# First weights issued from ScalarE's queue, and twelve buffers for raw inputs in an attention and Fourier filter kernel

## The chip, the cores and the metric

The kernel runs as one launch on one core of a Trainium2 chip. The metric is device time in microseconds (us) of one execution, as the median of several runs. Before the change it is 635.23 us, the median of 3 runs (634.75 to 635.24).

In the text PE is TensorE (PEld its weight loads), DVE is VectorE, ACT is ScalarE, POOL is GpSimd and SP is SyncE. SP computes nothing here; it issues DMAs. ACT and POOL can issue DMAs too, each from a queue of its own.

## What is computed

Two independent parts share the core, and their outputs are concatenated. Part A is attention with 16 heads of 28 channels, in which all heads share one key and one value head; part B filters an image of 2048 x 448 in the frequency domain.

```python
def _A_ref(x, wq, wk, wv, wo):
    q = (x @ wq).reshape(B, S, H, Dh).transpose(0, 2, 1, 3)
    k = x @ wk
    v = x @ wv
    scores = jnp.einsum("bhqd,bkd->bhqk", q, k) * (Dh ** -0.5)
    p = _softmax(scores, axis=-1)
    o = jnp.einsum("bhqk,bkd->bhqd", p, v)
    return o.transpose(0, 2, 1, 3).reshape(B, S, H * Dh) @ wo
...
def _B_ref(x, w_r, w_i):
    X = jnp.fft.rfft2(x, axes=(-2, -1)) * (w_r + 1j * w_i)
    return jnp.fft.irfft2(X, s=(S, D), axes=(-2, -1))
```

B is 1, S 2048, D 448, H 16 and Dh 28; all inputs are f32.

## The kernel before

The work has a start of some 70 us and a long main part. The main part (`PLAN`, line 48, and the loop at line 895) is written out by hand: PE computes scores (line 918), ACT takes their exponentials (853, 929, 943), PE multiplies them with the values (864), and the steps of the Fourier filter are set between them. The order on PE is the order of the program text in the whole kernel; the orders on DVE and ACT are fixed by hand only from line 506 on. Ahead of it a scheduler that comes with the language orders every other engine's instructions by its own estimate of when they can run.

The start, lines 257 to 502, makes the queries, keys and values. x is split in four columns of 512 positions (`c`), and its 448 channels in four blocks of 128 rows (`j`, `NK` = 4; the last block holds 64 channels twice). Matmuls in full f32 precision are put together from three products of numbers in a shorter format: `split_w` (335) makes the parts `wqh` and `wql` of a weight block, `split_x` (342) the parts `xh` and `xl` of an input block, `proj` (353) does the products. The high parts are casts, on ACT but for the very first block of x, which DVE casts (345). The low parts are differences on DVE (340, 349, 351). `evac` (361) writes a result to `qraw` on ACT and takes its largest magnitude on DVE (`qmx`, 364).

Every raw block lands in a buffer named `raw` of 128 x 512 f32 (256 KB), of which there are eight; a ninth load waits until the first buffer has been read. All raw loads are issued by SP, in this order: the first block of x (312); the first block of `wq` in three pieces of 128, 128 and 256 columns (321); the first block of the second column of x; then for j = 1, 2, 3 a block of x and the block of `wq` in two halves (328). Then come the rest of the second column, constants, the inputs `xb` and `fw` of the Fourier filter's first step (118, 120), and the third column of x.

A DMA is also given one of eight semaphores in turn, and it waits until the DMA that had the same semaphore before has landed. So at most eight DMAs of SP and ACT together are under way.

While the first loads are under way, ACT loads its function table and runs one exponential on a dummy (298), and PE runs 16 matmuls on zeros (305, `WARM` = 10, 6). PE's first real product is one of `xh` with the first piece of `wqh`; then one more matmul on zeros; then the products with `xl` and `wql`.

Beside the projections the start does the first step of the Fourier filter in eight parts: `fft1_fold` (123) adds and subtracts blocks of `xb` on DVE, PE multiplies the result (155), ACT copies it (161), PE multiplies again (174), and SP stores it (189). Near its end come four steps that lead to the first scores: `qm`, the largest magnitudes of the keys' part of `qraw` (459, DVE), with PE's `key_max` behind it (379); `prod` and `shift` (286, 291, 292), which make the constants `cvec`; `build_q(0, 0)`, three operations on DVE that make `ql`, `qh` and again `ql` (232, 234, 223); and `copy_q`, which spreads these over `qa` by DVE (210), ACT (208), SP and POOL (211). The first scores (918) read `qa`. POOL meanwhile fetches rows of keys and values to `kf` (273).

Of the kernel before, what the change touches and what calls it, by code (L numbers as in the profile page):

```python
# [10 lines left out]
F32 = mybir.dt.float32  # L11
# [54 lines left out]


WARM = 10, 6


@with_exitstack
def kernel(ctx: ExitStack, tc: tile.TileContext, t: dict):
    nc = tc.nc
# [183 lines left out]
    with tc.tile_pool(name="w1", bufs=1) as w1:  # L257
# [35 lines left out]

        halves = slice(0, 1024), slice(1024, 2048)
        with tc.tile_pool(name="x1", bufs=2) as x1:
            warm = x1.tile([1, 1], F32, name="warm")
            nc.vector.memset(warm, 0.0)
            nc.scalar.activation(warm, warm, AF.Exp)
# [3 lines left out]
            def zeros(n, nothing=None):  # L302
                nothing = bank() if nothing is None else nothing
                for _ in range(n):
                    mm(nothing[:, :256], idle[:, :128], idle, start=True, stop=True)

            for n in WARM:
                zeros(n)

            def raw(src, eng):  # L310
                r = x1.tile([128, 512], F32, name="raw", bufs=8)
                eng.dma_start(r, src)
                return r


            first = slice(0, 128), slice(128, 256), slice(256, 512)
            xr, wr = {}, {}
            xr[0, 0] = raw(t["xa"][0, :, 0], nc.sync)
            wr[0] = x1.tile([128, 512], F32, name="raw", bufs=8)
            for s in first:  # L320
                nc.sync.dma_start(wr[0][:, s], t["wq"][:, 0, s])

            xr[1, 0] = raw(t["xa"][1, :, 0], nc.sync)
            for j in range(1, NK):
                xr[0, j] = raw(t["xa"][0, :, j], nc.sync)
                wr[j] = x1.tile([128, 512], F32, name="raw", bufs=8)
                for s in (slice(0, 256), slice(256, 512)):
                    nc.sync.dma_start(wr[j][:, s], t["wq"][:, j, s])

# [647 lines left out]
    for k in range(4):  # L977
        divide(c, NG - 1, k)
        s = slice(128 * k, 128 * k + 128)
# [17 lines left out]
    with tc.If(rv > int(np.float32(BOUND).view(np.int32))), tc.tile_pool(name="g1", bufs=1) as g1:  # L997
# [13 lines left out]
        with tc.For_i(0, 64, 1) as n:  # L1011
# [3 lines left out]
            for i in range(4):  # L1015
                r = slice(32 * i, 32 * i + 32)
# [14 lines left out]
        with tc.For_i(0, NC, 1) as nq:  # L1031
            y = g1.tile([128, 4, D], F32, name="y")
            nc.vector.memset(y, 0.0)
            with tc.For_i(0, NG, 1) as ng:
# [5 lines left out]
                for i in range(4):  # L1040
                    r = slice(32 * i, 32 * i + 32)
# [145 lines left out]
```

## Time and profile before

| what | value |
| --- | --- |
| median of 3 runs | 635.23 us (634.75 to 635.24) |
| the profiled execution | 635.08 us |
| its span, first to last instruction | 633.3 us |
| granted clock of TensorE, mean | 1.00 |
| ACT, idle while PE computes what it evacuates at L363, 0 to 75 us | 15.4 us in 10 waits |
| ACT, idle for raw blocks of x (L347), 0 to 75 us | 4.6 us in 6 waits |
| ACT, idle for raw weights (L339), 0 to 75 us | 3.0 us in 4 waits |
| DVE, idle for the first block of x (L345) | 2.9 us |
| bytes moved by DMA | 66.74 MB, mean 105 GB/s |

Times in the rows of a profile are microseconds from the start of the span. A row in order of time gives the start, the length, the engine, the line, the operation, what is written and what is read, and in brackets the engine's idle time ahead of it with what ended it. "SPq", "ACTq" and "POOLq" rows are DMAs being issued; the data move later. A list of waits gives for each waiting line its releaser, the sum, the count and the longest wait. DMA share is the mean busy share of the 16 DMA engines.

### The profile page before, as it was taken

To read this page: it belongs to the slowest core of one execution; us is meant where nothing else is said; L and a number is where in the kernel's file an instruction comes from. 1 tells how busy PE (TensorE), PEld (TensorE's weight loads), DVE (VectorE), ACT (ScalarE), POOL (GpSimd) and SP (SyncE) were. 2 spreads that over 40 slices of the span, in tenths; PEclk is the share of its full clock that TensorE was granted. 3 is DMA by queue.
4 is the path that set the end of the run, shared out by engine and by line. 5 is a ranking of instruction groups with operands and counts; after the bars stand their busy time and mean duration, and the time that the engine had idled before them with its cause. 6 is when DMAs were issued, how large, how long until landed. Compare 5 with 4: busy or idle time off the path is not lost. (4 is left out here: it accounts for less than half of the span.)

```text
span 633.3 us, 12165 instructions
## 1 busy us (share of the span) xinstructions
PE 627.4 (99%) x4437; PEld 377.7 (60%) x4437; DVE 439.9 (69%) x793; ACT 546.9 (86%) x984; POOL 61.5 (10%) x118
## 2 busy tenths in 40 slices
PE   9999999999999999999999999999999999999997
PEld 7877645646565655646565665565566565555555
DVE  5999648789998943866766845277687764457653
ACT  5554999999999998988989989998989989989991
POOL 4021501011113110000110100001010100000000
PEclk9999999999999999999999999999999999999999
DMA  8865863456455522216340513034152413030011
GB/s 254 288 177 168 261 167 87 115 146 177 124 152 124 139 65 66 76 64 187 77 106 18 125 37 82 16 83 147 35 129 60 98 55 91 16 82 11 21 31 61
DMA packets 37891, 66.74 MB, mean 105 GB/s; under 512 B 8009, under 2 KB 22746, under 8 KB 36860
## 3 DMA queue, kind: packets, MB, share of 16 engines
q1 hardware_dynamic: 32608, 52.50, 30.2%
q0 software_dynamic: 4640, 12.48, 7.7%
q8 instruction: 36, 0.59, 0.4%
q10 hardware_dynamic: 576, 0.92, 0.4%
q14 instruction: 31, 0.25, 0.1%
HBM read 29.81 MB, written 17.87 MB: 75 GB/s over the span
## 5 line engine op out<-in xcount | busy, mean ns | idle before, releaser
L853 ACT ACTIVATE p<-s 128x512 f32<-128x512 f32 x405 | 222.1, 638 | 27.3 <-PE s L918 26.5
L918 PE MATMUL s<-qa,ka 128*128 128x512 f32 x756 | 227.6, 402 | 0.0
L918 PEld LDWEIGHTS s<-qa,ka 128*128 128x128 f32 x756 | 138.1, 188 | 60.9 <-issue 26.8
L924 DVE COPY k<-s 128x512 f32<-128x512 f32 x122 | 80.1, 684 | 62.9 <-PE s L918 62.7
L864 PE MATMUL s<-p,vs 128*32 128x512 f32 x976 | 121.3, 595 | 0.0
L853 ACT ACTIVATE qraw<-s 128x512 f32<-128x512 f32 x137 | 79.2, 655 | 6.5 <-PE s L918 6.5
L943 ACT ACTIVATE k<-k 128x1024 f32<-128x1024 f32 x80 | 83.5, 1145 | 0.0
L864 PEld LDWEIGHTS s<-p,vs 128*32 128x32 f32 x976 | 29.4, 109 | 64.3 <-issue 59.4
L918 PE MATMUL sx<-qa,ka 128*128 128x512 f32 x137 | 55.3, 403 | 0.0
L918 PE MATMUL po<-qa,ka 128*128 128x512 f32 x131 | 53.2, 406 | 0.0
L853 ACT ACTIVATE p<-po 128x512 f32<-128x512 f32 x75 | 48.2, 642 | 4.5 <-PE po L918 4.2
L864 PE MATMUL s<-qraw,vs 128*32 128x512 f32 x384 | 49.5, 593 | 0.0
L853 ACT ACTIVATE p<-sx 128x512 f32<-128x512 f32 x64 | 41.5, 649 | 3.0 <-PE sx L918 2.9
L738 POOL DMA_DIRECT2D ol<-ol x36 | 18.0, 508 | 229.0 <-DVE ol L761 156.9
L864 PE MATMUL s<-k,vs 128*32 128x512 f32 x304 | 39.7, 594 | 0.0
L918 PEld LDWEIGHTS sx<-qa,ka 128*128 128x128 f32 x137 | 25.7, 188 | 11.1 <-issue 4.2
L918 PEld LDWEIGHTS po<-qa,ka 128*128 128x128 f32 x131 | 24.6, 188 | 11.3 <-issue 5.0
L868 DVE STREAM_TRANSPOSE osb<-s 128x512 f32<-128x512 f32 x13 | 9.3, 716 | 28.0 <-PE s L864 27.9
L864 PEld LDWEIGHTS s<-qraw,vs 128*32 128x32 f32 x384 | 12.0, 110 | 27.3 <-issue 26.1
L924 DVE COPY k<-po 128x512 f32<-128x512 f32 x17 | 11.6, 685 | 21.4 <-PE po L918 21.3
L853 ACT ACTIVATE qraw<-sx 128x512 f32<-128x512 f32 x35 | 22.9, 653 | 2.0 <-PE sx L918 2.0
L924 DVE COPY p<-s 128x512 f32<-128x512 f32 x35 | 23.0, 681 | 0.0
(277 smaller groups left out, 973.5 us busy)
## 6 DMA issues: line engine op xcount, KB each, us to landing
qa<-qa SPq DMA_DIRECT2D x15, 512.0 KB
raw<-xa SPq DMA_DIRECT2D x16, 256.0 KB
xb<-xb SPq DMA_DIRECT2D x8, 512.0 KB
qa<-qh SPq DMA_DIRECT2D x64, 64.0 KB
qa<-ql SPq DMA_DIRECT2D x60, 64.0 KB
t<-bs SPq DMA_DIRECT2D x16, 225.0 KB
wr<-wr POOLq DMA_DIRECT2D x16, 225.0 KB, 3.8
wi<-wi POOLq DMA_DIRECT2D x16, 225.0 KB, 5.2
```

The costliest lines, as they stand in the source:

```text
L738: nc.gpsimd.dma_start(ol[c][o, g].bitcast(F32), ol[c][r, 0].bitcast(F32))
L853: nc.scalar.activation(tiles[-1][:, h % 2], sc, AF.Exp, scale=SCALE)
L864: mm(po[c, g][32 * i:32 * i + 32], vs[:, kc], ps[i // 2][:, i % 2], start=(n == 1), stop=(n == 16))
L868: nc.vector.transpose(o, po[c, g])
L918: begun.append(mm(sc, ka[:, kc * 128:(kc + 1) * 128], qa[c, g][:, h], start=True, stop=True))
L924: nc.vector.tensor_copy(keep[i][h // 2][:, h % 2], sc)
L943: nc.scalar.activation(p, p, AF.Exp, scale=SCALE)
```

## The change

The three pieces of the first weight block are issued from ACT's queue, as the first things that ACT does, in place of SP's. The constant `RAW` sets the number of `raw` buffers, twelve where there were eight.

```diff
+RAW = 12
...
         with tc.tile_pool(name="x1", bufs=2) as x1:
+            first = slice(0, 128), slice(128, 256), slice(256, 512)
+            xr, wr = {}, {}
+            wr[0] = x1.tile([128, 512], F32, name="raw", bufs=RAW)
+            for s in first:
+                nc.scalar.dma_start(wr[0][:, s], t["wq"][:, 0, s])
             warm = x1.tile([1, 1], F32, name="warm")
             nc.vector.memset(warm, 0.0)
             nc.scalar.activation(warm, warm, AF.Exp)
...
-                r = x1.tile([128, 512], F32, name="raw", bufs=8)
+                r = x1.tile([128, 512], F32, name="raw", bufs=RAW)
...
-            first = slice(0, 128), slice(128, 256), slice(256, 512)
-            xr, wr = {}, {}
             xr[0, 0] = raw(t["xa"][0, :, 0], nc.sync)
-            wr[0] = x1.tile([128, 512], F32, name="raw", bufs=8)
-            for s in first:
-                nc.sync.dma_start(wr[0][:, s], t["wq"][:, 0, s])
...
-                wr[j] = x1.tile([128, 512], F32, name="raw", bufs=8)
+                wr[j] = x1.tile([128, 512], F32, name="raw", bufs=RAW)
```

PE's order is the same. On the other engines the scheduler's order changes too. Lines in the rows of the change are higher by one in most places, since it adds a line in the middle of the program.

The beginning of ACT's order, before and then with the change (`wq` is the weight matrix in memory, `xa` the input, `wqh` and `xh` the high parts):

```order
L1183 UNCONDITIONAL_BRANCH
L298 ACT_TABLE_LOAD
L298 ACTIVATE warm<-warm 1x1
L339 ACTIVATE wqh<-raw 128x128 x2
L339 ACTIVATE wqh<-raw 128x256
```
```order
L1184 UNCONDITIONAL_BRANCH
L301 DMA raw<-wq 128x128 x2
L301 DMA raw<-wq 128x256
L304 ACT_TABLE_LOAD
L304 ACTIVATE warm<-warm 1x1
L340 ACTIVATE wqh<-raw 128x128 x2
L340 ACTIVATE wqh<-raw 128x256
```

The three issues stand ahead of the table load, and what follows is as it was. On SP they are gone, and the next loads follow the first block of x directly.

DVE's order at the first query, before and with the change (`cvec` holds the constants, `ql` and `qh` the parts of the query, the rows with `f` and `xb` are pieces of a fold, `qmx` a largest magnitude):

```order
L364 TENSOR_REDUCE qmx<-qraw 128x1
L292 COPY cvec<-s_89 128x4
L130 TENSOR_TENSOR f<-xb 113x16x32
L232 TENSOR_SCALAR ql<-qraw,mask,cvec 128x512
L130 TENSOR_TENSOR f<-xb 113x16x32
L234 CAST qh<-ql 128x512
L132 TENSOR_TENSOR xb<-f 113x512
L223 TENSOR_TENSOR ql<-ql,qh 128x512
L133 TENSOR_TENSOR xb<-f 113x512
```
```order
L365 TENSOR_REDUCE qmx<-qraw 128x1
L131 TENSOR_TENSOR f<-xb 113x16x32
L293 COPY cvec<-s_89 128x4
L131 TENSOR_TENSOR f<-xb 113x16x32
L233 TENSOR_SCALAR ql<-qraw,mask,cvec 128x512
L133 TENSOR_TENSOR xb<-f 113x512
L235 CAST qh<-ql 128x512
L134 TENSOR_TENSOR xb<-f 113x512
L224 TENSOR_TENSOR ql<-ql,qh 128x512
```

A piece of the fold moved from behind each of the four steps to ahead of it. Ahead of `qm` (459) DVE has the same instructions as before, some in another order.

POOL's order around the copies of `ql`, before and with the change (`kf` holds keys and values, `wr` a later weight of the filter):

```order
L273 DMA kf<-qraw 4x1536 x7
L273 DMA kf<-qraw 4x512 x5
L211 DMA qa<-ql 32x512 x2
L273 DMA kf<-qraw 4x512 x2
L211 DMA qa<-ql 32x512 x2
L593 DMA wr<-wr 64x900 x2
```
```order
L274 DMA kf<-qraw 4x1536 x7
L274 DMA kf<-qraw 4x512 x5
L212 DMA qa<-ql 32x512
L274 DMA kf<-qraw 4x512 x2
L212 DMA qa<-ql 32x512 x3
L594 DMA wr<-wr 64x900 x2
```

The last two fetches of `kf` now stand ahead of three of the four copies of `ql`, before ahead of two.

## The prediction

> **What bounds the kernel now.** I read the page first, for the shares of the engines, then the waits of PE, then the stretch from 0 to 70 us in order of time: the change lies there, and a wait that PE does not feel is worth nothing.
>
> ```profile
> span 633.3 us, 12165 instructions
> PE 627.4 (99%) x4437; PEld 377.7 (60%) x4437; DVE 439.9 (69%) x793; ACT 546.9 (86%) x984; POOL 61.5 (10%) x118
> ```
> ```profile
> PE s L305 <- DVE idle L301: 1.1, 1, 1.1
> PE s L379 <- DVE qm L459: 0.7, 1, 0.7
> ```
> ```profile
> 629.10 0.36 PE L971 MATMUL po<-wol,oh 128*128 128x448 f32 x1
> ```
>
> PE is idle for 633.3 - 627.4 = 5.9 us in all. Of this 633.3 - 629.46 = 3.8 us lie behind its last matmul (the last output), 1.1 us ahead of the first warm-up matmul, and 0.7 us in one hole at L379, where PE waits for DVE's `qm`. An earlier load can therefore win only the hole and what PE loses at its start. Those rows come next.
>
> ```profile
> 1.11 3.60 PE L305 MATMUL s<-idle 128*128 128x256 bf16 x16 [1.11 <-DVE idle L301]
> 4.51 0.29 PEld L359 LDWEIGHTS s<-xh,wqh 128*128 128x128 f32 x1 [0.28 <-ACT wqh L339]
> 4.52 0.72 PE L359 MATMUL s<-xh,wqh 128*128 128x512 f32 x1
> 5.16 0.50 PE L359 MATMUL s<-xl,wqh 128*128 128x512 f32 x1
> 5.50 0.40 PE L359 MATMUL s<-xh,wql 128*128 128x512 f32 x1
> 5.73 0.40 PE L359 MATMUL s<-xh,wqh 128*128 128x512 f32 x1
> 53.99 0.61 PE L379 MATMUL s<-qm,sel 128*128 128x1 f32 x4 [0.73 <-DVE qm L459]
> 69.64 2.24 PE L918 MATMUL s<-qa,ka 128*128 128x512 f32 x8
> ```
>
> The warm-ups hold PE from 1.11; the first real matmul starts at 4.52 and the second at 5.16; from 5.50 on they follow each other every 0.23 us, and the list of waits has nothing more until the hole that ends at 53.99. So in the first 54 us two chains run side by side: PE from its start, with 0.73 us to spare at the hole, and DVE up to `qm`, which decides when the hole ends. DVE's rows:
>
> ```profile
> 3.95 0.43 DVE L345 CAST xh<-raw 128x512 fp32r<-128x512 f32 x1 [2.90 <-DMA raw<-xa]
> 4.41 0.69 DVE L349 TENSOR_TENSOR xl<-raw,xh 128x512 fp32r<-128x512 f32 x1
> 15.76 0.69 DVE L351 TENSOR_TENSOR xh<-raw,xh 64x512 fp32r<-64x512 f32 x1 [0.44 <-ACT xh L347]
> 17.43 1.29 DVE L130 TENSOR_TENSOR f<-xb 113x512 f32<-113x512 f32 x2 [0.98 <-DMA xb<-xb]
> 53.78 0.16 DVE L459 TENSOR_REDUCE qm<-qmx 128x2 f32<-128x8 f32 x1
> ```
> ```profile
> 17.43:53.94 36.51, 35.84 (x485) 27.82 (x483) 36.28 (x69) 21.30 (x40) 5.08 (x10) 1.00 0.72 224
> ```
>
> The second fence is a stretch of the busy times (length, PE, PEld, DVE, ACT, POOL, clock, DMA share, GB/s): DVE works 36.28 of 36.51 us between the first fold at 17.43 and the end of `qm` at 53.94. It starts that run when `xb` lands, 0.98 us after its last work. Whatever brings `xb` earlier brings `qm` earlier, by up to 0.98 us and what the loads ahead of it gain too.
>
> **The change part by part.** *Three DMA issues leave SP and go ahead of ACT's table load.*
>
> ```profile
> 0.76 0.41 SPq L312 DMA_DIRECT2D raw<-xa  x1
> 1.23 1.36 SPq L321 DMA_DIRECT2D raw<-wq  x3
> ```
> ```profile
> 0.76 1.28 ACT L298 ACT_TABLE_LOAD   x1 [0.76 <-PEq L1177]
> 2.05 0.20 ACT L298 ACTIVATE warm<-warm 1x1 f32<-1x1 f32 x1
> 4.15 0.51 ACT L339 ACTIVATE wqh<-raw 128x128 fp32r<-128x128 f32 x2 [1.89 <-DMA raw<-wq]
> ```
> ```profile
> L784 ACTq DMA_DIRECT2D oa<-yb x4: 338/359/644, 624.7 to 630.4; - x4
> ```
>
> On ACT: 0.76 + 1.36 (three issues at SP's price) + 1.28 (table) + 0.20 = 3.60 us, ahead of the cast that now starts at 4.15. ACT's idle 1.89 us hides it; at the dearest issue seen on ACT (644 ns each) it would be 0.76 + 1.93 + 1.48 = 4.17, so this costs 0.0 us either way. The first piece is issued at 0.76 in place of 1.23 and can land 0.47 us earlier; SP's later loads are issued up to 1.36 us earlier.
>
> *What these issues buy at DMA.*
>
> ```profile
> 2.00:3.00 1.00, 1.00 (x6) 0.70 (x5) 0.00 (x0) 0.24 (x2) 0.94 (x2) 1.00 0.92 272
> 3.00:4.00 1.00, 1.00 (x6) 0.75 (x5) 0.05 (x1) 0.00 (x0) 1.00 (x3) 1.00 0.79 200
> 4.00:5.00 1.00, 1.00 (x5) 0.45 (x3) 0.97 (x2) 0.51 (x2) 1.00 (x2) 1.00 0.76 255
> 5.00:6.00 1.00, 1.00 (x6) 0.82 (x6) 0.75 (x4) 0.44 (x2) 0.03 (x1) 1.00 1.03 313
> ```
>
> The DMA share is 0.92, 0.79 and 0.76 in the three microseconds in which SP issues one small piece after another, and 1.03 once it has got ahead. From there the DMA engines, not the issues, set when bytes land. The 1.36 us are thus worth only what the engines idle: 0.08 + 0.21 + 0.24 = 0.53 us. `xb` stands behind the same bytes as before, so I let it land 0.5 us earlier. Bounds: 0 (another limit holds it) and 1.36 us. DVE then ends `qm` 0.5 us earlier.
>
> *PE's start.* `xa` no longer has the DMA engines to itself: the first piece of `wq` (128x128 f32, 64 KB) is issued in the same instant. At 272 GB/s 64 KB take 0.24 us, all three pieces (256 KB) 0.96 us. The chain behind `xa` is cast, `xl`, second matmul (3.95, 4.41 to 5.10, 5.16), so PE may start between 0.28 us earlier (the gap in front of the first real weights) and 0.96 us later. I take 0.25 us later, since only the first piece competes from the beginning. The hole hides it: 0.73 - 0.25 = 0.48 us are left, about what DVE gains. What is late next is PE itself.
>
> *Twelve buffers.*
>
> ```profile
> SPq L312 <- DVE wql L340: 0.8, 2, 0.4
> SPq L312 <- DVE xl L349: 0.7, 1, 0.7
> SPq L312 <- DVE xh L351: 0.4, 1, 0.4
> ```
> ```profile
> 19.70 2.04 ACT L347 ACTIVATE xh<-raw 128x512 fp32r<-128x512 f32 x3 [0.99 <-DMA raw<-xa]
> ```
>
> Before, SP waited 0.8 + 0.7 + 0.4 = 1.9 us for DVE to free buffers, all ahead of the third column's loads, which stand behind the first `xb` in the queue. Their first user is ACT at 19.70, after 0.99 us of waiting, and no wait of PE hangs on it: worth 0 us here, and at most those 0.99 us if PE had no cover.
>
> *What the scheduler moved elsewhere.* On DVE each step of the first query (`cvec`, `ql`, `qh`, `ql`) now stands behind one more piece of a fold; on POOL two key fetches stand ahead of three copies of `ql`, not of two.
>
> ```profile
> 59.86 0.68 DVE L130 TENSOR_TENSOR f<-xb 113x512 f32<-113x512 f32 x1
> 62.46 0.68 DVE L223 TENSOR_TENSOR ql<-ql,qh 128x512 fp32r<-128x512 f32 x1
> ```
> ```profile
> 63.43 1.03 POOL L211 DMA_DIRECT2D qa<-ql  x2 [3.27 <-DVE ql L223]
> 65.47 1.20 POOL L211 DMA_DIRECT2D qa<-ql  x2
> ```
> ```profile
> DMA to landing us min/median/max: 2.8/3.9/4.3
> ```
>
> One such piece takes DVE 0.6 us from start to start, so `ql` ends 0.6 us later against PE, and POOL's last copy is issued at about 66.6, not 66.0 (65.47 and half of the first pair's 1.03). With 2.8 to 3.9 us to its landing that is 69.4 to 70.5. PE's fourth score, the one that reads it, starts at 69.64 + 3 x 0.23 = 70.3. The cost lies between 0 and 0.6 us; I take 0.1, as most of that interval is still in time.
>
> *Sum.* DVE's chain gives -0.5, PE's own -0.73 + 0.25 = -0.48; the later of the two counts, -0.48, and +0.1 makes -0.4 us. The profiled execution took 635.08 us (span 633.3, the other 1.8 around it), near the median of 635.23 (634.75 to 635.24). 635.08 - 0.4 = **634.7 us**: a gain on paper, and no change that can be told, for I call anything within 0.2% (1.27 us, so 633.96 to 636.50) the same.
>
> **The rivals.** *A, the start moves too.* If the pieces land 0.47 us earlier and `xa` no later, the 0.28 us in front of the first weights go as well, and with a full 0.98 us on DVE the hole closes: -0.28 - 0.73 = -1.0, or 634.1; with the second matmul 0.4 us earlier still, 633.7. For it: PE's gap is ended by `wqh`. Against it: the second matmul hangs on `xa`, not on `wq`.
>
> *B, nothing comes of it.* `xb` lands when it did, or the 0.5 us are given back at the first scores (their upper bound, 0.6): 635.08 to 635.3, say 635.2. For it: the DMA share from 5 us on. [...]
>
> [...]
>
> That the pieces stay where they were is excluded: ACT's order has them first.
>
> **How the numbers follow.** The forecast 0.40 (633.8 to 635.0), A 0.22, B 0.24, C 0.14. Faster by over 0.2%: 0.15 of A and 0.05 of the forecast's lower end, 0.20. Slower: 0.13 of C. Same: the rest, 0.67. The range goes from A's early end, 633.6, to 636.3, which leaves out most of C and little else.
>
> **What would show it.** In the profile after: ACT's table load at about 2.1 and its first cast at or before 4.15; DMA share near 1 from 2 to 5 us; DVE's first cast at 4.1 to 4.3 (4.9 would be C); the first fold at about 16.9; PE's wait for `qm` near 0 to 0.2 us; the eight scores still in 2.24 us with no wait ahead. A first fold at 17.4 would make this wrong for B, a first real matmul ahead of 4.4 for A. A shift that arises after 75 us would make it wrong as a whole, for nothing here reaches so far.

## The result, and the profile after

The changed kernel takes 635.73 us in the median of 22 runs (634.82 to 638.1), the kernel before in runs next to it 634.99 (634.14 to 636.75, 22 runs). The ratio is 1.0016 with a 95% interval of 1.001 to 1.0022: slower by about 1.0 us by that ratio, and by 0.74 us between the medians, for some runs of the change come late and weigh in the ratio. The forecast was 634.7, a small gain; the time lies inside the range, on the other side of no change. The profiled execution after took 635.9 us, the one before 635.08. Single executions of 698, 782 and 1608 us occurred among the runs below; ranges, counts and ratios leave them out.

The page and the list of PE's waits after (line, releaser, sum, count, longest, in us):

```profile
span 634.1 us, 12161 instructions
PE 627.1 (99%) x4437; PEld 377.4 (60%) x4437; DVE 440.5 (69%) x793; ACT 546.8 (86%) x984; POOL 60.8 (10%) x118
```
```profile
PE s L311 <- DVE idle L307: 1.1, 1, 1.1
PE s L360 <- DVE xh L346: 0.7, 1, 0.7
PE s L360 <- ACT wqh L340: 0.5, 1, 0.5
PE s L775 <- DMA oh<-ol: 0.4, 1, 0.4
```

The wait for `qm`, the hole of 0.7 us, is gone as forecast. In its place PE waits 0.7 us for the first `xh` and 0.5 us for a weight. PE in order of time, after, and two rows of before that the prediction did not show (the first product with the third piece, and the first of `pq`):

```profile
5.20 0.47 PE L360 MATMUL s<-xh,wqh 128*128 128x512 f32 x1 [0.72 <-DVE xh L346]
5.83 0.50 PE L360 MATMUL s<-xl,wqh 128*128 128x512 f32 x1
6.17 0.40 PE L360 MATMUL s<-xh,wql 128*128 128x512 f32 x1
6.41 0.40 PE L360 MATMUL s<-xh,wqh 128*128 128x512 f32 x1
...
7.56 0.50 PE L360 MATMUL s<-xh,wqh 128*128 128x512 f32 x1 [0.52 <-ACT wqh L340]
...
9.27 0.39 PE L360 MATMUL pq<-xh,wqh 128*128 128x512 f32 x1
...
54.64 0.61 PE L380 MATMUL s<-qm,sel 128*128 128x1 f32 x4
...
70.24 2.24 PE L919 MATMUL s<-qa,ka 128*128 128x512 f32 x8
...
629.62 0.36 PE L972 MATMUL po<-wol,oh 128*128 128x448 f32 x1
```
```profile
6.19 0.39 PE L359 MATMUL s<-xh,wqh 128*128 128x512 f32 x1
...
7.80 0.39 PE L359 MATMUL pq<-xh,wqh 128*128 128x512 f32 x1
```

PE's first product is 0.68 us late (5.20, before 4.52), the first with the third piece 1.37 (7.56, before 6.19). When PE turns to the second column of x (`pq`) it is 1.47 us late (9.27, before 7.80). It is 0.65 us late behind the old hole (54.64, before 53.99), 0.60 at the first scores and 0.52 at the last matmul. Set beside each other one by one, the matmuls of the two profiles are 1.44 to 1.47 us apart from 10 us to the hole and 0.60 at 100 us; the new wait at L775 (at 368 us) makes it 0.84, and by 443 us it is 0.55. So the loss arises ahead of 9.3 us, the hole pays half of it, and the rest is carried to the end. The span grew by 0.8; the missing 0.3 us lie behind the last matmul, in the last output, and were not followed up.

ACT and SP at the start, after ("ACTq" and "SPq" rows are issues):

```profile
0.76 1.39 ACTq L301 DMA_DIRECT2D raw<-wq  x3
2.18 1.28 ACT L304 ACT_TABLE_LOAD   x1 [2.18 <-issue]
3.48 0.20 ACT L304 ACTIVATE warm<-warm 1x1 f32<-1x1 f32 x1
4.72 0.31 ACT L340 ACTIVATE wqh<-raw 128x128 fp32r<-128x128 f32 x1 [1.04 <-DMA raw<-wq]
5.76 0.31 ACT L340 ACTIVATE wqh<-raw 128x128 fp32r<-128x128 f32 x1 [0.73 <-DMA raw<-wq]
7.09 0.42 ACT L340 ACTIVATE wqh<-raw 128x256 fp32r<-128x256 f32 x1 [1.02 <-DMA raw<-wq]
```
```profile
0.76 1.36 SPq L318 DMA_DIRECT2D raw<-xa  x3
2.17 0.91 SPq L329 DMA_DIRECT2D raw<-wq  x2
```

ACT is free again at 3.68 and then waits for data, so the table load was hidden. But the pieces, issued at 0.76 to 2.15 in place of 1.23 to 2.59, are cast at 4.72, 5.76 and 7.09. Before, two were cast in one row from 4.15 and the third here:

```profile
5.30 0.42 ACT L339 ACTIVATE wqh<-raw 128x256 fp32r<-128x256 f32 x1 [0.65 <-DMA raw<-wq]
```

Issued earlier, the third piece landed 1.8 us later. SP meanwhile issues three blocks of x by 2.12 and the next weight block by 3.08. DVE's rows after:

```profile
4.54 0.52 DVE L346 CAST xh<-raw 128x512 fp32r<-128x512 f32 x1 [3.49 <-DMA raw<-xa]
...
16.79 1.56 DVE L131 TENSOR_TENSOR f<-xb 113x512 f32<-113x512 f32 x2 [1.21 <-DMA xb<-xb]
...
53.49 0.16 DVE L460 TENSOR_REDUCE qm<-qmx 128x2 f32<-128x8 f32 x1
```

The first block of x is cast 0.59 us later (4.54, before 3.95); `xb`, far back in SP's queue, is there 0.64 us earlier (16.79, before 17.43), and `qm` is made 0.29 earlier (53.49, before 53.78). The stretches (columns as in the prediction, DMA share next to last):

```profile
2.00:3.00 1.00, 1.00 (x6) 0.69 (x5) 0.00 (x0) 0.82 (x1) 0.95 (x2) 1.00 0.68 196
3.00:4.00 1.00, 1.00 (x6) 0.75 (x5) 0.00 (x0) 0.67 (x2) 1.00 (x3) 1.00 1.00 237
4.00:5.00 1.00, 0.48 (x4) 0.13 (x2) 0.46 (x1) 0.28 (x1) 0.80 (x2) 1.00 0.95 303
```

From 3 us on the DMA share is 0.95 to 1.00 (the forecast had the engines full from 2 us on, where the share is 0.68); their time goes to other loads than the ones that PE waits for. Counting the rows that they moved in the trace's DMA records, by queue and by the microsecond in which a row began, shows to which:

```
after       ACT's queue (the pieces)    SP's queue (x, then the next weights)
2 to 3 us   75 rows of 512 B            77 rows of 2048 B
3 to 4 us   67 rows of 512 B            99 rows of 2048 B
4 to 5 us   109 of 512 B, 17 of 1024 B  112 rows of 2048 B
5 to 6 us   5 of 512 B, 92 of 1024 B    84 of 2048 B, 60 of 1024 B
```

Over these four microseconds the two queues got 365 and 432 rows, near one for one. A row of SP's x has 2048 bytes and one of the first two pieces 512, so ACT's queue moved 0.24 MB in that time and SP's 0.82 MB. In the kernel before, the 256 rows of the first two pieces were moved in a row, from 2.62 to 3.92 us; now they take from 2.14 to 5.23. The small records of 4 bytes that end each load, 16 of them, show the same: those of the first block of x and of the first piece come in 16 pairs, each 5 to 6 ns apart (the first at 2.937 and 2.943 us, the last at 4.101 and 4.107), although the rows of the one load took 84 ns each and those of the other 27. How one DMA engine divides its time between the queues is not shown, for the records name no engine.

### The profile page after: what moved, and what is told of

Same layout as the page of the kernel before. It is cut to its first block, busy times and chain, and to the rows that moved or that the text cites. A ratio compares the mean times of both kernels' runs of the same rounds, so it can differ in the third digit from the quotient of the medians.

```text
span 634.1 us, 12161 instructions
## 1 busy us (share of the span) xinstructions
PE 627.1 (99%) x4437; PEld 377.4 (60%) x4437; DVE 440.5 (69%) x793; ACT 546.8 (86%) x984; POOL 60.8 (10%) x118
## 5 line engine op out<-in xcount | busy, mean ns | idle before, releaser
L360 PE MATMUL s<-xh,wqh 128*128 128x512 f32 x56 | 22.7, 405 | 1.2 <-DVE xh L346 0.7
```

Of the source, the lines that this page charges most:

```text
L360: mm(pq, w[:, j, gs], x[:, j], start=(j == 0 and n == 0), stop=(j == 3 and n == 1))
```

## The experiments

The first theory, from these rows: the pieces on ACT's queue share the DMA engines (365 of the 797 rows counted above) with loads that SP now issues up to 1.4 us earlier, and PE waits for them. Its rivals: the twelve buffers or the scheduler's new order cost the time, or PE's clock does (the clock theory: PE's gap ahead of its first product goes with a longer stretch of slow matmuls and with the late runs; a conjecture, which two of the kernels below try). One more, on the size of the rows, came later. All comparisons are of 11 runs of a kernel (in one case 5) with 28 or 34 of the kernel before. The row to read in each profile is the first matmul that writes `pq`: 7.80 before, and 0.73 us later costs nothing, since the hole pays.

**The change with eight buffers.**

```diff
-RAW = 12
+RAW = 8
```

> The change with eight buffers again (only the issue moved). Theory 1 (the second and third piece on ACT's queue share the DMA engines with the loads that SP now issues 1.4 us earlier, so the weights land late and PE loses 1.4 us of which the hole at key_max returns 0.7): as slow as the change, 635.5 to 636.0 in the median, with PE's two waits at L360 (0.7 and 0.5 us) and no hole at L380. Theory 2 (the twelve buffers or the order that the scheduler makes with them cost it): back at the time before, 635.0, within 0.2 us.

635.59 us (635.04 to 638.76) against 634.92, ratio 1.0022 (1.0009 to 1.0035). PE in that profile:

```profile
7.45 0.50 PE L360 MATMUL s<-xh,wqh 128*128 128x512 f32 x1 [0.38 <-ACT wqh L340]
...
9.17 0.39 PE L360 MATMUL pq<-xh,wqh 128*128 128x512 f32 x1
```

The loss is there without the buffers, with the same late third piece; PE's two waits are 0.3 and 0.4 us, smaller than expected. Two more facts belong to it: four of its runs lie above 637 us, so that its ratio shows twice the loss of its median, and on DVE, ACT and POOL it has the new order of the change.

**The kernel before with twelve buffers.**

```diff
-                r = x1.tile([128, 512], F32, name="raw", bufs=8)
+                r = x1.tile([128, 512], F32, name="raw", bufs=12)
```

> The kernel before with twelve buffers (all issues stay on SP). Theory 1: as before, 635.0 within 0.2 us, first real matmul near 4.5 and the hole of 0.7 us still there. Theory 2: 635.5 or more.

634.71 us (634.37 to 635.56) against 634.92, 0.9997 (0.9988 to 1.0005): nothing that can be measured. The two kernels together put the loss on the move of the issues and what comes with it. That is also the new order, since this kernel has the order of before and the one with eight buffers has that of the change. The order is excluded by the rows after: PE's delay is complete at 9.3 us, grows no more up to the hole, and the first scores have no wait. This profile also shows a late third piece, by less, for a reason that was not followed:

```profile
6.34 0.42 ACT L339 ACTIVATE wqh<-raw 128x256 fp32r<-128x256 f32 x1 [1.77 <-DMA raw<-wq]
```
```profile
8.55 0.40 PE L359 MATMUL pq<-xh,wqh 128*128 128x512 f32 x1
```

PE is 0.75 us late at `pq`, what the hole pays (it was expected to stay, but PE has no wait there), and the time is that of before.

**Only the first piece on ACT, the other two on SP behind x.**

```diff
-            for s in first:
-                nc.scalar.dma_start(wr[0][:, s], t["wq"][:, 0, s])
+            nc.scalar.dma_start(wr[0][:, first[0]], t["wq"][:, 0, first[0]])
...
             xr[0, 0] = raw(t["xa"][0, :, 0], nc.sync)
+            for s in first[1:]:
+                nc.sync.dma_start(wr[0][:, s], t["wq"][:, 0, s])
```

> The change, but only the first of the three pieces is issued by ACT; the other two follow the first block of x on SP as before. Theory 1: the third piece is cast by 5.5 again (7.1 in the change) and PE's wait of 0.5 us is gone; xa shares with 64 KB only, so the first real matmul starts at 4.5 to 4.9; median 634.6 to 635.2. If sharing with the first piece alone makes xa late (rival 3): first real matmul near 5.2 as in the change, median 635.2 to 635.5.

634.87 us (634.23 to 635.59) against 634.92, 0.9998 (0.9989 to 1.0006). ACT's casts and `pq`:

```profile
3.76 0.31 ACT L341 ACTIVATE wqh<-raw 128x128 fp32r<-128x128 f32 x1 [1.08 <-DMA raw<-wq]
4.34 0.31 ACT L341 ACTIVATE wqh<-raw 128x128 fp32r<-128x128 f32 x1 [0.27 <-DMA raw<-wq]
5.79 0.42 ACT L341 ACTIVATE wqh<-raw 128x256 fp32r<-128x256 f32 x1 [1.15 <-DMA raw<-wq]
```
```profile
8.56 0.39 PE L361 MATMUL pq<-xh,wqh 128*128 128x512 f32 x1
```

With one piece beside `xa`, the first cast comes earlier than in the kernel before and x hardly later (its cast at 4.02); the third cast, at 5.79, misses the expected 5.5. `pq` is 0.76 us late here as well, although the first product is late by only 0.12 (4.64): matmuls are still 0.42 us apart at 6 us and come down to 0.23 us at 6.72, before at 5.50. The hole pays it. This is the case that the prediction priced, a first piece alone beside `xa`, at 0.25 us; it gains nothing, and the loss of the change is gone with the second and third piece back on SP.

**The change with three tiny loads on SP behind the first block of x**, 128 x 1 from `mask`, which nothing reads, so that SP's later loads are issued no earlier than before.

```diff
             xr[0, 0] = raw(t["xa"][0, :, 0], nc.sync)
+            for _ in range(3):
+                nc.sync.dma_start(x1.tile([128, 1], F32, name="pad", bufs=3), t["mask"])
```

> The change with three tiny loads (128x1 f32, unused) on SP between the first block of x and the next loads, so that these are issued no earlier than before the change, with the three pieces on ACT. Theory 1: nothing but the first block of x stands beside the pieces; third piece cast by 5.0, first real matmul 4.4 to 4.8, no second wait of PE; median 634.7 to 635.4. If the place of the issue as such (ACT's queue) is slow (rival 4): the third piece is still cast near 7, and the median is 635.5 to 636.

635.21 us (634.59 to 636.66) against 634.92, 1.0007 (0.9998 to 1.0015): between the two, and not to be told from either. The profile says more. ACT and PE here, then PE of before:

```profile
4.11 0.67 ACT L342 ACTIVATE wqh<-raw 128x128 fp32r<-128x128 f32 x2 [0.45 <-DMA raw<-wq]
5.75 0.42 ACT L342 ACTIVATE wqh<-raw 128x256 fp32r<-128x256 f32 x1 [0.96 <-DMA raw<-wq]
```
```profile
8.71 0.50 PE L362 MATMUL pq<-xh,wqh 128*128 128x512 f32 x1 [0.38 <-ACT xh L350]
9.43 0.50 PE L362 MATMUL pq<-xl,wqh 128*128 128x512 f32 x1 [0.22 <-DVE xl L352]
...
10.00 0.39 PE L362 MATMUL po<-xh,wqh 128*128 128x512 f32 x1
```
```profile
8.48 0.39 PE L359 MATMUL po<-xh,wqh 128*128 128x512 f32 x1
```

With the same pieces on the same queue, but SP's later loads held back, the casts return from 4.72, 5.76 and 7.09 to 4.11 (two) and 5.75. So it is these loads that delay the pieces here, as the first theory says. Not all of it comes back: a third cast by 5.0 and a first product by 4.8 were expected, and they came at 5.75 and 4.88, with `xa` and the tiny loads' own rows still beside the pieces. Now the held-back loads are late themselves: PE waits twice for the second block of x, and at `po` it is 1.52 us late (10.00, before 8.48).

**The change with four more warm-ups on PE**, 20 in place of 16, so that its gap is filled.

```diff
-WARM = 10, 6
+WARM = 10, 10
```

> The change with four more matmuls on zeros (WARM = 10, 10), which close PE's gap ahead of the first real matmul. [...]

635.36 us (634.83 to 636.24) against 634.93, 1.0007 (0.9998 to 1.0016). In the profile nothing is won, for the data are as late:

```profile
7.54 0.50 PE L360 MATMUL s<-xh,wqh 128*128 128x512 f32 x1 [0.49 <-ACT wqh L340]
...
9.27 0.39 PE L360 MATMUL pq<-xh,wqh 128*128 128x512 f32 x1
```

The median lies between those of the change and of before. What changes is the upper end of the runs: 4 of 22 runs of the change and 4 of 11 of its form with eight buffers lie above 637 us, none of these 11 do, and none of the 84 of the kernel before. With 0 of 11 this points to the gap and does not prove it.

**The kernel before with four warm-ups fewer**, which makes a gap without moving a load. Near the first query the scheduler's order changes on DVE and POOL; there both fetches of `kf` now stand ahead of the last copy of `ql` alone.

```diff
-WARM = 10, 6
+WARM = 10, 2
```

> The kernel before with four matmuls on zeros less (WARM = 10, 2), so that PE idles about 1 us ahead of its first real matmul while the loads stay as they were. Clock theory: several of 11 runs come 1 to 3 us later (636 to 638), which the kernel before did in 0 of 34 runs; the others stay at 635.0. Rival: all within 634.1 to 635.8.

636.39 us in the median against 634.93, 1.0015 (1.0005 to 1.0025); the runs lie from 633.87 to 637.29, 8 of 11 above the highest run of the kernel before beside it (635.61). The profile is of the slowest, 637.29 us:

```profile
4.45 0.79 PE L359 MATMUL s<-xh,wqh 128*128 128x512 f32 x1 [0.59 <-ACT wqh L339]
...
6.12 0.63 PE L359 MATMUL s<-xh,wqh 128*128 128x512 f32 x1
6.55 0.63 PE L359 MATMUL s<-xl,wqh 128*128 128x512 f32 x1
...
8.26 0.63 PE L359 MATMUL s<-xl,wqh 128*128 128x512 f32 x1
...
9.65 0.39 PE L359 MATMUL pq<-xh,wqh 128*128 128x512 f32 x1
9.88 0.40 PE L359 MATMUL pq<-xl,wqh 128*128 128x512 f32 x1
...
72.85 1.39 PE L918 MATMUL s<-qa,ka 128*128 128x512 f32 x5 [1.23 <-ACT k L929]
```

The first product starts when it did before (4.45), yet the matmuls follow each other every 0.43 us and come down to 0.23 only at about 9.6; before, they did so from 5.50. In this profile a gap of 0.59 us in the warm-up goes with 1.85 us at `pq`; that it spares other runs is read from their times alone. In the kernel with one DMA below, whose gap is 1.95 us, they come down at 9.95, in all others between 5.39 and 6.72. The trace's record of PE's granted clock, full from its beginning, begins at 5.03 us in the kernel before and at 4.11 in the change (the clock column of the stretches reads 1.00 ahead of that as well). So the change's gap of 0.72 us, from 4.48 to 5.20, lies behind that beginning; what makes the pace late in two profiles of ten is not shown.

The slow pace, 0.43 us up to about 9 us, goes with only half of this run's loss. PE is 1.06 us late behind the hole; the last row above is a second wait, at the first scores, and behind it PE is 2.4 us late. The profile names ACT as its releaser; SP's copies of `qh`, which the scores read too, were issued until 69.50 us, before until 65.63. Which of the two it was, and whether the gap or the new order made it, is not shown.

**The first weight block as one DMA on ACT's queue.** In the counts above the two queues got rows near one for one; if they do so again, an estimate from those counts, rows of 2048 bytes take an even share of the bytes and land sooner. For that the median was put at 634.9 to 635.5 and the end of the third cast at 6.0 or earlier.

```diff
-            for s in first:
-                nc.scalar.dma_start(wr[0][:, s], t["wq"][:, 0, s])
+            nc.scalar.dma_start(wr[0], t["wq"][:, 0])
```

> The change with the 256 KB of the first weight block issued by ACT as one DMA of 2 KB rows, not as pieces of 512 B and 1 KB rows. [...]

637.52 us (637.09 to 637.68, 5 runs) against 634.93, 1.004 (1.0027 to 1.0054): the slowest of all. ACT, DVE and PE:

```profile
5.89 0.82 ACT L339 ACTIVATE wqh<-raw 128x128 fp32r<-128x128 f32 x3 [3.21 <-DMA raw<-wq]
```
```profile
6.08 0.43 DVE L345 CAST xh<-raw 128x512 fp32r<-128x512 f32 x1 [5.03 <-DMA raw<-xa]
```
```profile
6.66 0.77 PE L359 MATMUL s<-xh,wqh 128*128 128x512 f32 x1 [1.95 <-DVE xh L345]
...
11.11 0.40 PE L359 MATMUL pq<-xh,wqh 128*128 128x512 f32 x1
```

The expectation fell: the time is 2.0 us above its range, and the third cast (6.31 to 6.71) ends later than 6.0. It is earlier than in the change (7.09), but nothing can start before the whole block and `xa` have landed, and both were there only at about 6 us: `xa` is cast 2.13 us later than before, the gap grows to 1.95 us, and the matmuls stay at 0.43 us to about 9.7. Why two loads of 512 KB in all took until then stays open.

**The exchange: x on ACT's queue, the pieces first on SP's.**

```diff
             for s in first:
-                nc.scalar.dma_start(wr[0][:, s], t["wq"][:, 0, s])
+                nc.sync.dma_start(wr[0][:, s], t["wq"][:, 0, s])
+            xr[0, 0] = x1.tile([128, 512], F32, name="raw", bufs=RAW)
+            nc.scalar.dma_start(xr[0, 0], t["xa"][0, :, 0])
...
-            xr[0, 0] = raw(t["xa"][0, :, 0], nc.sync)
```

> The first block of x goes to ACT's queue and the three pieces stay on SP, now as its first issues, with the rest of SP's loads behind them. Theory 1: only these 512 KB share, SP's later loads come after the pieces in its own queue; first real matmul at 4.4 to 5.0 when xa is there, third piece cast by 5.5, no second wait, first fold 0.3 us earlier; median 634.5 to 635.2. If sharing as such costs what the change cost: 635.5 or more.

634.98 us (634.23 to 636.97) against 634.93, 1.0003 (0.9994 to 1.0011).

```profile
8.32 0.39 PE L361 MATMUL pq<-xh,wqh 128*128 128x512 f32 x1
```

One issue in place of three leaves SP, and SP's later loads again stand behind the pieces. The third cast is at 5.62, PE has a short second wait (0.30 us, for `xl`), and `pq` is 0.52 us late, less than the hole pays; the time is that of before.

Side by side, from one profile and one median each. "Beyond the hole" is the delay at `pq` less 0.73 us (at `po` where PE still waits inside `pq`); the last column is the median less that of the kernel before beside it:

| kernel | first `pq` | beyond the hole | median less before |
| --- | --- | --- | --- |
| x on ACT's queue | 8.32 | none | +0.05 |
| before, twelve buffers | 8.55 | 0.02 | -0.21 |
| one piece on ACT | 8.56 | 0.03 | -0.05 |
| change, eight buffers | 9.17 | 0.64 | +0.67 |
| the change | 9.27 | 0.74 | +0.74 |
| change, 20 warm-ups | 9.27 | 0.74 | +0.43 |
| change, SP held back | `po` 10.00 | 0.79 | +0.29 |
| before, 12 warm-ups | 9.65 | 1.12 | +1.46 |
| one DMA on ACT | 11.11 | 2.58 | +2.59 |

The three kernels that stay within the hole, or pass it by 0.03 us at most, cost nothing; the others cost about what they go beyond it, within 0.5 us. This sets one profile beside a median, so it is a rough agreement: the matmuls come down to 0.23 us anywhere from 5.39 to 9.95 us, and the profile with 12 warm-ups is of a run 2.2 us longer than that of before, of which the start explains 1.1. No version tried beats the kernel before by more than the measurement can tell.

## Why the prediction was wrong

*What bounds the kernel* held: PE is busy for 99% in both, and what it loses at its start, less the hole, is what the kernel loses.

*ACT's issues and table load, 0.0 us*: right. Three issues took 1.39 us, and ACT waited for data at every cast.

*DVE's chain, -0.5 us*: near at its source (the first fold 0.64 us earlier), but `qm` came only 0.29 earlier, so a part of it was lost on the way. The reason given was misread, so that the size met is partly luck: SP issued the pieces from 1.23 to 2.59 us, and in the stretches from 2 to 5 us, with shares of 0.92 to 0.76, it was already issuing whole blocks of x and halves of weights. What the DMA engines moved then was to a good part short rows: from 2 to 4 us 256 rows of 512 B and 103 of 1024 B, beside 115 of 2048 B.

*PE's start, +0.25 us*: the step that failed, and with it the sign. It measured +0.68 at the first product and +1.47 at `pq`. The working let only "the first piece" compete with `xa` and counted bytes at the full rate. Two things were left out. The two queues got near the same number of rows (365 and 432 from 2 to 6 us), and with rows of 512 and 1024 B beside rows of mostly 2048 B the pieces got 0.24 of 1.07 MB. And the prediction itself had SP's later loads issued up to 1.36 us earlier, counted that as a gain for `xb`, and did not ask what those loads would stand beside: the second and third piece, which PE needs first. The kernel with SP held back shows this second part. The lateness of x itself is split only roughly: its cast is 0.07 us late with one piece beside it, 0.36 with three pieces and SP held back, and 0.59 in the change, each from one profile; by an estimate, the first piece's 128 rows of 512 B at 27 ns, spread over 16 engines, make 0.2 us, and the rest is open. The upper bound of 0.96 us for the start held for the first product, but no bound was set for the later pieces, and the third had little slack: its cast ended at 5.72 before, and its first product ran at 6.19. Landing 1.8 us later, it held PE up.

*The hole pays 0.73 us*: right, and the reason why 1.47 us at `pq` became 0.65 behind it. Corrected, the sum is PE's own +1.47 - 0.73 = +0.74 us, with nothing more for DVE: 635.08 + 0.74 = 635.8, beside a profiled 635.9. That it is so close is partly luck: PE's last matmul is 0.52 us late, and the other 0.3 us arose behind it. The change with eight buffers has no such addition (0.47 late at the last matmul, its run 0.42 us longer than that of before).

*Buffers, 0 us*: right, by both experiments on them. *The later copies of `ql`, +0.1 (0 to 0.6)*: nothing; the eight scores still take 2.24 us with no wait.

*The rivals.* A (the start earlier) fell with the first cast, 0.57 us late. B put the limit rightly at the DMA engines and stopped at "nothing". Hardly any bandwidth came of the second queue (267 GB/s from 2 to 6 us in the mean, before 260), and the issue time saved went to the wrong loads. C, with its chance of 0.14, was a slower kernel by a longer slow pace of PE's matmuls behind a later `xa`; how long a gap keeps them slow was the author's estimate, and no run shows the term. What the runs showed: in the change's profile the gap is 0.72 us, but the record of the full clock begins at 4.11 us, ahead of the gap (4.48 to 5.20), matmuls follow each other every 0.23 us from 6.17 on, and the loss is late data; with a gap of 0.59 us and loads as before the matmuls are 0.43 us apart up to about 9 us, and PE is 1.1 us late beyond the hole. Such a slow pace would fit the runs of the change above 637 us; that it makes those runs was not seen in a profile of one.

## What to carry to other kernels

Moving a load to a second queue also brought forward everything behind it in the first queue: here SP's next loads were issued up to 1.4 us earlier, stood beside the second and third piece, and these were cast at 5.76 and 7.09 us, where one queue had both by 5.30. Before doing so, list the loads in the order in which the bounding engine needs them, and ask of each what will stand beside it, in rows and not only in bytes (365 rows beside 432 were 0.24 MB beside 0.82 here). Where the bounding engine has a hole further on, a delay up to its size (0.73 us) was free here and only about the excess counted.

## What was not expected of the hardware

- Two queues got 365 and 432 rows in 2 to 6 us, though the rows of one were 512 or 1024 bytes and of the other mostly 2048: near one row for one, so that the load cut into narrow pieces got 0.24 of 1.07 MB. The 256 rows of the first two pieces took 3.1 us in place of 1.3.
- With a gap of 0.59 us in PE's warm-up the matmuls are 0.43 us apart in a profile up to about 9 us and come down to 0.23 only by 9.65, in place of 5.50; behind a gap of 0.72 us in another, where the record begins at 4.11 us, ahead of the gap, they are 0.23 us apart from 6.17 on.
